# Second channel matmul of batch 1 in seven products of quarters, the u turns issued ahead of the last q turns, and a shifted PSUM bank count

## The chip, the cores and the metric

The kernel runs on one core of a Trainium2 chip. The metric is the device time of one execution in microseconds (us), as the median over several executions. The core's engines are called by the profile's names: PE (TensorE, matmuls) and PEld (its weight loads), DVE (VectorE), ACT (ScalarE), POOL (GpSimd) and SP (SyncE, which here only issues DMAs).

## What is computed

Eight batches, eight heads, 576 tokens, head size 64. A linear attention with cosine weights makes x; an MLP mixer with a token part and a channel part follows.

```python
q_p, k_p = phi(q), phi(k)             # relu(x) * cos_w and relu(x) * sin_w, side by side: 128 features
kv  = einsum('bhsf,bhsd->bhfd', k_p, v)
z   = sum(k_p, axis=2)
num = einsum('bhsf,bhfd->bhsd', q_p, kv)
den = einsum('bhsf,bhf->bhs', q_p, z)[..., None] + 1e-06
x   = (num / den).transpose(0, 2, 1, 3).reshape(8, 576, 512)
h   = maximum(x.transpose(0, 2, 1) @ w_tok1, 0) @ w_tok2      # 576 -> 256 -> 576
u   = x + h.transpose(0, 2, 1)
out = u + maximum(u @ w_ch1, 0) @ w_ch2                       # 512 -> 1536 -> 512
```

Inputs and output are float32; the matmuls take bfloat16 and add up in float32.

## The kernel before

**Groups and stages.** The 576 tokens of a batch are four blocks of 128 and a tail of 64. The MLP of a batch works on the four blocks (512 tokens); the eight tails of 64 make a ninth group (g = 8). A head part of the program does batch 0 and most of the work ahead of batch 1. Then comes the loop `for g in range(1, B + 1)` (L977), one **stage** for each group. In stage g, PE runs the channel MLP of group g. In between, the attention of batch b = g + 1 is finished, its token MLP is done, and the features of batch f = g + 2 are prepared.

**Steps.** The order of all instructions is written out by hand. `plan_of(g)` (L920) gives a list of steps, and `put(s, fn, ...)` hangs work on step s. Each step first issues a piece of the MLP on PE and then what hangs on it, in the order of the `put` calls. Steps 0 to 11 are the first channel matmul: one of twelve tiles of h1T (128 rows of the hidden layer by 512 tokens) with four matmuls of 512 columns (`mlp1`, L316), which `mlp1_out` (L328 on ACT, L330 on DVE) takes through relu into `h1T`. Every engine works through its own instructions in the order of the program; DMAs that SP issues wait in SP's order too.

**Second channel matmul, two forms.** In stage 1 (and for batch 0) it is plain: `mlp2` (L334) does, for each of four token blocks, twelve matmuls of 512 columns, in three steps of four, and `mlp2_out` (L339, DVE) adds u. From stage 2 on it has a form with seven products of quarters (Strassen's scheme in Winograd's form): the two dimensions h1T x w_ch2 are halved, `t_sum` makes T1 to T4 from the four quarters B11, B12, B21, B22 of w_ch2 once, `s_sums` makes S1 to S4 from the quarters of h1T in each stage (four DVE instructions for each range of chunks c, L358 to L361), and `mlp2_unit` (L378) does 14 units of six matmuls of 256 columns, two for each product. `mlp2_sums` adds the products up: a copy on ACT (L399), six additions on DVE (L401 to L430) and six additions of u on POOL (L396, in three pairs).

**Where S and T lie.** They use buffers of raw inputs that are free by then: S1 to S3 in `raw["k"][1]`, T3 and T4 in `raw["q"][1]`, S4 in `raw["v"][1]`. Batches 1 and 3 are the only ones loaded into the buffers [1]; all others go to [0].

**PSUM.** `psM` has four banks, handed out in turn by `nextM()` (count `cnt["M"]`), for MLP tiles and products; `psA` has two double banks for everything else.

**The turns.** Features of q (`qfeat`, L137 on ACT, L139 on DVE) are turned into `qpT` by a transposing DMA on SP (`qturn_dma`, L161), one for each of five token blocks j. u is cast to bfloat16 on ACT (`u_cast`, L264) and turned into `uT` by two such DMAs (`uturn_dma`, L269). All of `uT` of a batch must be there before the first MLP tile of its stage. For batch 1, ahead of the loop, u is turned on PE instead, into two psM banks, and copied out by DVE (`uturn_out`, L283, shown as L155). `tail_turn` (L304) turns the tails of u.

**Other work in the plan.** `f1k` makes one half of the K features of a block (which 0 with cos, 1 with sin) on a given engine; `vcast` casts v on POOL (L155); `kv_step` (L182) does kv for a block, `num_step` num (L201, L205) and x (L218 to L222), `b1_step` and `u_step` the token MLP (L232 to L259). `q_load`, `k_load`, `v_load` issue the loads of a later batch on SP (L131). `flush` issues the stores of results on POOL.

Of the kernel before, what the change touches and what calls it, by code (L numbers as in the profile page):

```python
# [18 lines left out]
def kernel(  # L19
# [77 lines left out]
    def views(t, m):  # L97
        b, n = t.rearrange("p h n d -> p (h n d)").bitcast(BF16), NQ * DQ
        return [b[:, i * n:(i + 1) * n].rearrange("p (c d) -> p c d", c=NQ) for i in range(m)]

    T1, T2 = [sb(f"w_ch2_t{i}", [P, NQ, DQ], BF16) for i in (1, 2)]
    T3, T4 = views(raw["q"][1], 2)
    S1, S2, S3 = views(raw["k"][1], 3)
    S4, = views(raw["v"][1], 1)
# [248 lines left out]
    def s_sums(c0, c1):  # L353
        V = nc.vector
        s1, s2, s3, s4 = [x[:, c0:c1, :] for x in (S1, S2, S3, S4)]
# [4 lines left out]
        V.tensor_sub(s3, a11, a21)  # L360
        V.tensor_sub(s4, a12, s2)  # L361
# [3 lines left out]
    def mlp2_unit(g, i):  # L365

        pr, tt = divmod(i, 2)
        a, w, bank = ((h1T[:, 0:NQ, 0:2 * P], B11, "A"), (S2, T2, "X"), (S3, T3, "F"), (S1, T1, "E"),
# [487 lines left out]
    uturn_out(1, 1, uturn_mm(1, nextM()), V)  # L856
    p(2, 3)
# [12 lines left out]
    order_of = lambda g: range(NCH) if g == 1 else (0, 6, 1, 7, 2, 8, 3, 9, 4, 5, 10, 11)  # L870
# [49 lines left out]
    def plan_of(g):  # L920
        b, f = g + 1, g + 2
        NS = 24 if g == 1 else 26
        plan = [[] for _ in range(NS)]

# [3 lines left out]
        if g == 1:  # L928
            put(5, tail_step, 1)
            put(19, tail_turn, 1)  # L930
            for j in range(NJ):
                put(j // 2 + 1, f1k, b, j, 0, V)
                put((j + 1) // 2 + 2, kv_step, b, j)
                put(5 + j, num_step, b, j)
            put(3, u_out, 1, 1)
            for n in range(2):
                put(10 + n, b1_step, b, n)
                put(13 + n, u_step, b, n)
                put(13 + n, uturn_step, b, n)
            for j in range(NJ):  # L940
                put(8 + j, f1k, f, j, 1, A)
                put(10 + j, f1k, f, j, 0, V)
                put(8 + j, vcast, f, j, G)
                put(18 + j, kv_step, f, j)
            for j, at in enumerate((12, 15, 16, 17, 18)):
                put(at, q_step, f, j)
            for i in range(4):
                put(19 + i, t_sum, i)
            put(8, v_load, 4)
            put(20, q_load, 4)  # L950
            put(22, k_load, 4)
            return plan
# [8 lines left out]
        for at, cs in ((7, (0, 2)), (9, (2, 4)), (11, (4, 5))):  # L961
            put(at, s_sums, *cs)
        if f < B:
            for j in range(NJ):
                put((7, 8, 10, 12, 13)[j], qfeat, f, j, V, A)
                put((7, 8, 10, 12, 13)[j], qturn_dma, f, j)
# [10 lines left out]
    for g in range(1, B + 1):  # L977
        mps = {}
        plan = plan_of(g)
        order = order_of(g)  # L980
        for s in range(len(plan)):
            if s < NCH:
                ps = mlp1(g, order[s])
            elif g == 1:
                t, part = divmod(s - NCH, 3)
                if part == 0:
                    mps[t] = nextM()
                mlp2(g, t, part, mps[t])
            else:
                mlp2_unit(g, s - NCH)  # L990
                mlp2_sums(g, s - NCH)
# [42 lines left out]
```

## Time and profile before

| what | value |
|---|---|
| median of 4 runs | 266.46 us (265.88, 266.26, 266.66, 267.33) |
| the profiled execution | 265.88 us, span from first to last instruction 264.1 us |
| granted PE clock | 1.00 throughout |
| stage 1, tiles of the first matmul | starts 57.81, ends 73.66 |
| stage 1, second matmul | 73.66 to 86.96 |
| first MLP tile of stages 4, 5, 6 | 140.17, 168.21, 195.86 |
| PE's last group of matmuls starts | 259.96 |

How to read the profile: times in a timeline are us from the start of the span; a line there gives start, duration, engine, source line, operation, written and read tiles, and how many instructions are merged in it. In brackets stands how long the engine had been idle before it, and what ended the wait. The wait table gives for engine and tile the releaser, the idle time in total, how many times, and the longest. "SPq" is SP's queue of DMA issues; there the duration is that of issuing. A line number can be that of a helper: every cast or copy on POOL or DVE has L155, every feature L137 or L139.

Busy time in a few stretches (us; of the stretch's length):

| stretch | PE | weight loads | DVE | ACT | POOL |
|---|---|---|---|---|---|
| 57.80 to 73.66 (stage 1, first half) | 15.79 of 15.86 | 7.98 | 12.25 | 9.02 | 4.25 |
| 73.66 to 86.96 (stage 1, second half) | 13.19 of 13.30 | 6.70 | 11.26 | 8.15 | 1.78 |
| 100.90 to 114.10 (stage 2, second half) | 13.20 of 13.20 | 10.44 | 11.61 | 9.10 | 5.08 |
| 140.00 to 168.00 (stage 4) | 26.89 of 28.00 | 17.03 | 23.42 | 18.10 | 11.90 |
| 168.00 to 196.00 (stage 5) | 26.48 of 28.00 | 17.19 | 21.45 | 16.75 | 10.24 |

### The profile page before, as it was taken

How to read it: one execution, taken by the hardware profiler on the slowest of the kernel's cores; microseconds unless marked ns; L12 is line 12 of the kernel's file. 1: busy time of each engine (PE TensorE's matmuls, PEld its weight loads, DVE VectorE, ACT ScalarE, POOL GpSimd, SP SyncE). 2: the span in 40 equal slices, each digit the busy share in tenths (PEclk: the TensorE clock that was granted, in tenths of full speed). 3: DMA queues.
4: the chain of work that ended last, by engine and by line, in shares of the span. 5: the costliest groups of instructions: out<-in, count | busy, mean ns of one | idle time of the engine just before them, and what ended most of it. 6: DMA issues, size and time to landing. Idle time of an engine off the chain costs nothing. (4 is left out here: it accounts for less than half of the span.)

```text
span 264.1 us, 5726 instructions
## 1 busy us (share of the span) xinstructions
PE 252.3 (96%) x2122; PEld 153.3 (58%) x2138; DVE 191.8 (73%) x447; ACT 148.4 (56%) x246; POOL 99.0 (37%) x172
## 2 busy tenths in 40 slices
PE   7799999989999999999999999899989999999994
PEld 2565456445445546864695468555855476486483
DVE  5883886696869689859985999398937783463563
ACT  4763685875666549646864687357825442612610
POOL 4196657070312510540545073604290135036032
PEclk9999999999999999999999999999999999999999
DMA  6999999999968999799968995899961035103004
GB/s 202 368 376 392 387 390 379 288 198 359 362 175 198 213 305 185 152 255 316 274 126 243 378 232 82 214 367 255 142 194 71 0 76 130 56 0 122 39 0 161
DMA packets 79948, 57.20 MB, mean 217 GB/s; under 512 B 48176, under 2 KB 74928, under 8 KB 79920
## 3 DMA queue, kind: packets, MB, share of 16 engines
q1 hardware_dynamic: 76128, 47.26, 67.3%
q0 software_dynamic: 2560, 8.39, 8.0%
q10 hardware_dynamic: 1232, 1.18, 1.4%
q8 instruction: 17, 0.28, 0.4%
q14 instruction: 11, 0.09, 0.1%
HBM read 35.85 MB, written 9.44 MB: 171 GB/s over the span
## 5 line engine op out<-in xcount | busy, mean ns | idle before, releaser
L316 PE MATMUL psM<-uT,w_ch 128*128 128x512 bf16 x368 | 88.2, 379 | 3.3 <-DMA uT<-u_bf 2.3
L328 ACT ACTIVATE h1T<-psM 128x512 bf16<-128x512 f32 x93 | 55.4, 597 | 45.5 <-PE psM L316 43.6
L316 PEld LDWEIGHTS <-w_ch 128*128 128x128 bf16 x416 | 37.5, 97 | 43.7 <-issue 5.0
L396 POOL TENSOR_TENSOR res<-res,u_sb 128x256 f32<-128x256 f32 x36 | 26.7, 772 | 52.5 <-DVE res L401 46.5
L155 POOL CAST vb<-v_raw 128x512 bf16<-128x512 f32 (+1 forms) x43 | 25.4, 633 | 52.8 <-DMA v_raw<-in_v_dram 52.5
L137 ACT ACTIVATE kp<-k_raw,sin_t 128x512 bf16<-128x512 f32 (+1 forms) x45 | 28.1, 666 | 1.3 <-DMA k_raw<-in_k_dram 1.3
L137 ACT ACTIVATE qp<-q_raw,sin_t 128x512 bf16<-128x512 f32 (+1 forms) x40 | 26.3, 681 | 2.8 <-DMA q_raw<-in_q_dram 2.8
L378 PEld LDWEIGHTS <-k_raw 128*128 128x128 bf16 x252 | 24.4, 98 | 5.1 <-issue 1.2
L378 PEld LDWEIGHTS <-h1T 128*128 128x128 bf16 x252 | 23.9, 98 | 5.3
L334 PE MATMUL psM<-w_ch,h1T 128*128 128x512 bf16 x90 | 22.7, 379 | 0.2
L139 DVE TENSOR_SCALAR kp<-k_raw,cos_t 128x512 bf16<-128x512 f32 (+1 forms) x45 | 21.0, 494 | 1.8 <-DMA k_raw<-in_k_dram 1.8
L378 PE MATMUL psM<-w_ch,h1T 128*128 128x256 bf16 x168 | 22.1, 273 | 0.0
L259 DVE TENSOR_TENSOR u_sb<-psA,x_sb 128x1024 f32<-128x1024 f32 x16 | 19.4, 1215 | 2.1 <-PE psA L254 1.9
L378 PE MATMUL psM<-w_ch_t,k_raw 128*128 128x256 bf16 x162 | 20.5, 273 | 0.0
L222 DVE TENSOR_TENSOR x_sb<-psA,rden 128x512 bf16<-128x512 f32 x28 | 19.4, 691 | 1.0
L358 DVE TENSOR_TENSOR k_raw<-h1T 128x512 bf16<-128x512 bf16 (+1 forms) x28 | 10.3, 370 | 11.8 <-ACT h1T L328 11.1
L139 DVE TENSOR_SCALAR qp<-q_raw,cos_t 128x512 bf16<-128x512 f32 (+1 forms) x40 | 17.3, 464 | 1.4 <-DMA q_raw<-in_q_dram 1.4
L218 DVE TENSOR_SCALAR rden<-psA 128x8 f32<-128x8 f32 x35 | 5.7, 163 | 16.2 <-PE psA L201 15.0
L254 PE MATMUL psA<-B,w_tok 128*128 128x512 bf16 x63 | 16.4, 379 | 0.1
L444 POOL DMA_DIRECT2D out_dram<-res x16 | 8.9, 558 | 19.5 <-DVE res L339 14.2
L201 PEld LDWEIGHTS <-qpT 128*128 128x128 bf16 x256 | 11.8, 98 | 7.6 <-issue 1.2
L232 PE MATMUL psA<-x_sb,w_tok 128*128 128x512 bf16 x50 | 14.1, 379 | 0.6 <-DVE x_sb L222 0.3
(139 smaller groups left out, 372.3 us busy)
## 6 DMA issues: line engine op xcount, KB each, us to landing
out_dram<-res POOLq DMA_DIRECT2D x32, 256.0 KB, 4.4
k_raw<-in_k_dram SPq DMA_DIRECT2D x7, 640.0 KB, 9.4
v_raw<-in_v_dram SPq DMA_DIRECT2D x7, 640.0 KB, 10.8
q_raw<-in_q_dram SPq DMA_DIRECT2D x7, 640.0 KB, 6.9
k_raw<-in_k_dram SPq DMA_DIRECT2D x7, 512.0 KB, 7.8
v_raw<-in_v_dram SPq DMA_DIRECT2D x7, 512.0 KB, 10.4
q_raw<-in_q_dram SPq DMA_DIRECT2D x7, 512.0 KB, 4.6
u_sb<-in_moe_w_ch_dram SPq DMA_DIRECT2D x2, 1024.0 KB, 10.2
```

The costliest lines, as they stand in the source:

```text
L137: eng.activation(out_ap, in_ap, AF.Relu, bias=0.0, scale=s)
L139: eng.tensor_scalar(out_ap, in_ap, scalar1=s, scalar2=0.0, op0=ALU.mult, op1=ALU.max)
L155: eng.tensor_copy(out_ap, in_ap)
L222: nc.vector.tensor_mul(dst.rearrange("p (g h d) -> p g h d", g=2, h=HH), n[:, :, :, 0:D], rb)
L232: nc.tensor.matmul(ps[mi], w1[:, j, mi * P:(mi + 1) * P], x_sb[:, j, :], start=(mi == 0 and j == 0), stop=(mi == 1 and j == T - 1), skip_g ...
L254: nc.tensor.matmul(ps[:, half, :], w2[:, ki, 2 * c + half, :], B1[b % 2][:, ki, :], start=(ki == 0), stop=(ki == NT - 1))
L259: nc.vector.tensor_add(u_sb[b % 2][:, 2 * c:2 * c + 2, :], ps, x_sb[:, 2 * c:2 * c + 2, :])
L316: nc.tensor.matmul(ps.rearrange("p (t k) -> p t k", k=P), wc1[:, ki, mi * P:(mi + 1) * P], src[:, :, ki, :], start=(ki == 0), stop=(ki == ...
L328: eng.activation(h1T[:, mi, :], ps, AF.Relu)
L334: nc.tensor.matmul(ps, h1T[:, ki, t * P:(t + 1) * P], wc2[:, ki, :], start=(ki == 0), stop=(ki == NCH - 1))
L378: nc.tensor.matmul(m[tt][:, tt, :], a[:, c, tt * P:(tt + 1) * P], w[:, c, :], start=(pr < 4 and c == 0 and (tt == 0 or own)), stop=(c == N ...
L396: G.tensor_add(c[:, t, :], s[:, t, :], u[:, t, :])
```

## The change

1. Stage 1 takes the form of seven products too: its plan grows from 24 to 26 steps, its first matmul follows the order of the other stages (0, 6, 1, 7, ...), the plain form of `mlp2` remains for batch 0 alone.
2. For that, T1 to T4 are made within stage 1 (steps 3, 4, 12 and 17, where they were at 19 to 22), T3 = B22 - B12 is written over B12, and S and T get other places: `rows_of(t, i)` takes a quarter-run of 256 elements out of each of six rows of a raw buffer and leaves the fifth block of a row alone. In stage 1, S1 and S2 lie in `raw["k"][0]` and S3 in `raw["q"][0]`; later in the buffers [1]. S4 and T4 lie in `raw["v"][1]` always.
3. Around it, the plan of stage 1 changes: `vcast` of batch 3 at step 5; K features with sin at 9 to 11; the turns of u at 15 and 16 (13 and 14 before); Q features and turns of batch 3 at 12, 13, 20, 21, 22 (12, 15 to 18 before), K features with cos at 15, 15, 19, 20, 21, both for blocks 0 and 1 on ACT instead of DVE; `kv_step` of batch 3 at 20, 21, 22, 24, 25; `q_load(4)` at 22 (20 before).
4. In stages 2 to 5, the DMAs that turn q blocks 3 and 4 go from steps 12 and 13 to step 17, behind the two turns of u at steps 15 and 16; their features stay where they were.
5. `cnt["M"] += 2` after the two turns of u for batch 1: every later tile takes the psM bank two further on.

```diff
-    def views(t, m):
-        b, n = t.rearrange("p h n d -> p (h n d)").bitcast(BF16), NQ * DQ
-        return [b[:, i * n:(i + 1) * n].rearrange("p (c d) -> p c d", c=NQ) for i in range(m)]
+
+    def rows_of(t, i):
+        b = t.rearrange("p h n d -> p h (n d)").bitcast(BF16)
+        return b[:, 0:NQ, i * DQ:(i + 1) * DQ]
 
     T1, T2 = [sb(f"w_ch2_t{i}", [P, NQ, DQ], BF16) for i in (1, 2)]
-    T3, T4 = views(raw["q"][1], 2)
-    S1, S2, S3 = views(raw["k"][1], 3)
-    S4, = views(raw["v"][1], 1)
+    T3 = B12
+    S4, T4 = [rows_of(raw["v"][1], i) for i in range(2)]
+    S_of = [[rows_of(raw["k"][i], 0), rows_of(raw["k"][i], 1), rows_of(raw["q"][i], 0), S4] for i in range(2)]
...
     uturn_out(1, 0, uturn_mm(0, nextM()), V)
     uturn_out(1, 1, uturn_mm(1, nextM()), V)
+    cnt["M"] += 2
     p(2, 3)
...
             put(3, u_out, 1, 1)
+            for i, at in enumerate((3, 4, 12, 17)):
+                put(at, t_sum, (0, 1, 3, 2)[i])
+            for j in range(NJ):
+                put((9, 10, 10, 11, 11)[j], f1k, f, j, 1, A)
             for n in range(2):
                 put(10 + n, b1_step, b, n)
                 put(13 + n, u_step, b, n)
-                put(13 + n, uturn_step, b, n)
+                put(15 + n, uturn_step, b, n)
+            put(10, s_sums, g, 0, 3)
+            put(11, s_sums, g, 3, 5)
             for j in range(NJ):
-                put(8 + j, f1k, f, j, 1, A)
-                put(10 + j, f1k, f, j, 0, V)
-                put(8 + j, vcast, f, j, G)
-                put(18 + j, kv_step, f, j)
-            for j, at in enumerate((12, 15, 16, 17, 18)):
-                put(at, q_step, f, j)
-            for i in range(4):
-                put(19 + i, t_sum, i)
+                put((12, 13, 20, 21, 22)[j], qfeat, f, j, (A, A, V, V, V)[j], A)
+                put((12, 13, 20, 21, 22)[j], qturn_dma, f, j)
+                put((15, 15, 19, 20, 21)[j], f1k, f, j, 0, (A, A, V, V, V)[j])
+                put(5, vcast, f, j, G)
+                put((20, 21, 22, 24, 25)[j], kv_step, f, j)
             put(8, v_load, 4)
-            put(20, q_load, 4)
+            put(22, q_load, 4)
             put(22, k_load, 4)
...
                 put((7, 8, 10, 12, 13)[j], qfeat, f, j, V, A)
-                put((7, 8, 10, 12, 13)[j], qturn_dma, f, j)
+                put((7, 8, 10, 17, 17)[j], qturn_dma, f, j)
...
             if s < NCH:
-                mlp1_out(order[s], ps, V if s in ((11,) if g == 1 else (10,)) else A)
-                if g > 1 and s == NCH - 1:
-                    s_sums(NQ - 1, NQ)
-            elif g == 1 and part == 2:
-                mlp2_out(g, t, mps[t], False)
+                mlp1_out(order[s], ps, V if s == 10 else A)
+                if s == NCH - 1:
+                    s_sums(g, NQ - 1, NQ)
```

More of the change, by code (lines that the diff above doesn't have):

```diff
@@ L351, in t_sum, with s_sums @@
             V.tensor_sub(T3, B22, B12)
-    def s_sums(c0, c1):
+    def s_sums(g, c0, c1):
         V = nc.vector
-        s1, s2, s3, s4 = [x[:, c0:c1, :] for x in (S1, S2, S3, S4)]
+        s1, s2, s3, s4 = [x[:, c0:c1, :] for x in S_of[min(g, 2) - 1]]
         a11, a21 = h1T[:, c0:c1, 0:2 * P], h1T[:, c0:c1, 2 * P:4 * P]
@@ L367, in mlp2_unit @@
         pr, tt = divmod(i, 2)
+        S1, S2, S3, S4 = S_of[min(g, 2) - 1]
         a, w, bank = ((h1T[:, 0:NQ, 0:2 * P], B11, "A"), (S2, T2, "X"), (S3, T3, "F"), (S1, T1, "E"),
@@ L866 @@
         load(3, src_of[n], n, (SY, SY))
-    order_of = lambda g: range(NCH) if g == 1 else (0, 6, 1, 7, 2, 8, 3, 9, 4, 5, 10, 11)
+    order = (0, 6, 1, 7, 2, 8, 3, 9, 4, 5, 10, 11)
     def kv_step(b, j):
@@ L921, in plan_of @@
         b, f = g + 1, g + 2
-        NS = 24 if g == 1 else 26
-        plan = [[] for _ in range(NS)]
+        plan = [[] for _ in range(26)]
         def put(s, fn, *args):
@@ L961, in plan_of @@
         for at, cs in ((7, (0, 2)), (9, (2, 4)), (11, (4, 5))):
-            put(at, s_sums, *cs)
+            put(at, s_sums, g, *cs)
         if f < B:
@@ L977 @@
     for g in range(1, B + 1):
-        mps = {}
         plan = plan_of(g)
-        order = order_of(g)
         for s in range(len(plan)):
@@ L983 @@
                 ps = mlp1(g, order[s])
[L984 to L988, printed above, removed]
             else:
```

## The prediction

> **What bounds the kernel now.** I read the busy shares first, then the waits of PE, then PE's timeline where it idles, and last the queues that set those idle moments.
>
> ```profile
> PE 252.3 (96%) x2122; PEld 153.3 (58%) x2138; DVE 191.8 (73%) x447; ACT 148.4 (56%) x246; POOL 99.0 (37%) x172
> PE psM L316 <- DMA uT<-u_bf: 2.3, 2, 1.3
> PE psM L316 <- DVE res L339: 0.7, 1, 0.7
> PE psM L316 <- DVE res L420: 0.2, 1, 0.2
> ```
>
> PE is busy 96% of the span, and from stage 1 on its only waits are these three, 3.2 us together (columns: sum, times, longest). So the time falls by what PE no longer has to issue and by these waits, and by little else. Where they lie:
>
> ```profile
> 57.81 2.75 PE L316 MATMUL psM<-uT,w_ch 128*128 128x512 bf16 x12 [0.73 <-DVE res L339]
> 140.17 2.75 PE L316 MATMUL psM<-uT,w_ch 128*128 128x512 bf16 x12 [0.21 <-DVE res L420]
> 168.21 2.75 PE L316 MATMUL psM<-uT,w_ch 128*128 128x512 bf16 x12 [1.09 <-DMA uT<-u_bf]
> 195.86 2.75 PE L316 MATMUL psM<-uT,w_ch 128*128 128x512 bf16 x12 [1.26 <-DMA uT<-u_bf]
> ```
>
> All stand at the head of a stage (1, 4, 5, 6), before its first MLP tile. The whole second half of stage 1 (73.66 to 86.96) runs without a wait.
>
> **The products (a gain of 1.19).** Stage 1 drops 48 matmuls of 512 columns and gets 14 units of six matmuls of 256, 84 in all. The chain of waits has both counts as uninterrupted runs:
>
> ```profile
> 231.91 9.17 PE psM L378 x84
> 241.08 10.36 PE psM L316 x48
> ```
>
> 10.36 - 9.17 = 1.19 us less on PE (216 against 109 ns each). The 36 further weight loads lie under matmuls: in the second half of stage 2, made of these units, PE's loads are busy 10.44 of 13.20 us, and PE is busy throughout.
>
> The Trainium skill has a rule against this edit: "TensorE: Matmul & The Clock Gate", section Back-to-back issue gap, says that in a stream of load and matmul a 512-column matmul costs about 131 ns and a 128-column one about 81, so halving the columns saves much less than half. By it (an estimate, 98 ns for 256 columns) the edit would be 84 x 98 - 48 x 131 = 1.9 us dearer. The trace's 216 and 109 ns contradict the rule, and I go by the trace.
>
> **The other bank (0.60).** Before stage 1, PE's last matmul of batch 0 ends at 57.08. The two copies of the turned u (DVE, 55.84 for 1.32) end at 57.16. Then comes L339, whose first addition frees the bank of tile 0, and PE starts at 57.81.
>
> ```profile
> 55.84 1.32 DVE L155 COPY uT<-psM 128x1024 bf16<-128x1024 bf16 x2
> 57.08 1.28 DVE L339 TENSOR_TENSOR res<-psM,u_sb 128x512 f32<-128x512 f32 x2
> ```
>
> With the count moved by two, tiles 0 and 1 take the banks of the turned u, free at 56.5 and 57.16. The start becomes 57.16 + 0.05 = 57.21, a gain of 0.60. The banks behind L339 now hold tiles 2 and 3, wanted at 58.9 and 59.8; L339 is done at 58.36. Late next is the K feature of batch 2 (DVE, 59.41 to 59.88), which PE wants at 59.81: 0.1 lost.
>
> **Turns of u before the last q turns (2.35).** Stage 5:
>
> ```profile
> 186.93 1.03 ACT L264 CAST u_bf<-u_sb 128x1024 bf16<-128x1024 f32 x1
> 188.49 1.03 ACT L264 CAST u_bf<-u_sb 128x1024 bf16<-128x1024 f32 x1
> 187.27 1.23 SPq L161 DMA_TRANSPOSE qpT<-qp  x1
> 189.19 1.23 SPq L161 DMA_TRANSPOSE qpT<-qp  x1
> 190.52 2.23 SPq L269 DMA_TRANSPOSE uT<-u_bf  x1
> 192.87 1.24 SPq L269 DMA_TRANSPOSE uT<-u_bf  x1
> ```
>
> The casts end at 187.96 and 189.52, but SP issues in order, and q turn 4 waited for its DVE feature until 189.19. The second u turn is issued at 192.87 and lands at 195.73 (2.86 later). Put first, it issues at 189.55 and lands at 192.4; PE is ready at 194.60. The wait of 1.26 goes, with 2.2 to spare. Likewise stage 4: casts end at 159.9 and 161.9, landing 164.7 against PE at 167.12; 1.09 goes. Stage 2 had no such wait. The 0.21 ahead of stage 4 is between nothing (bank) and 0.21 (that u turn, issued 137.27, lands near 140.1); I take nothing. What is late next is L416, which frees the bank of the next first tile: 193.41 + 0.61 = 194.02, in time by 0.6.
>
> The q turns themselves now go out at about 190.9 and 192.2 and land 3.0 to 6.5 later (the view of the q turns' line gives 4.2 as median), 198.7 at worst; PE wants turn 3 at 200.7 and turn 4 at 201.8. The q and v loads behind them in SP's queue leave at the same time as before, since the same four turns stand ahead. POOL's queue is untouched there. K loads, though, follow SP while the stages shrink, so they come up to 1.1 closer to their features; ACT is then late by at most that, within the 2.2 spare of the u turn.
>
> **Stage 1 rearranged (a loss of 0.7).** DVE gets 12 sums of quarters, six additions of 0.6 in place of four, and gives back four features to ACT. Its list from the end of the last x (70.32, which is 70.92 less 0.6): sums of chunks 0 to 2 1.96 (from 1.48 for a set of four at 512 columns and 1.0 at 256, in stage 2), MLP tile 0.61, sums 1.48 and 1.0, T3 and T4 0.95 each, two u 1.14 each, six additions 3.66, six features 2.4: 15.3, so to 85.6, where PE ends at 85.2. No slack is left, and POOL's casts of v sit on the first sums:
>
> ```profile
> 70.48 3.26 POOL L155 CAST vb<-v_raw 128x512 bf16<-128x512 f32 x5 [10.75 <-DMA v_raw<-in_v_dram]
> 155.16 0.69 DVE L360 TENSOR_TENSOR k_raw<-h1T 128x256 bf16<-128x256 bf16 x1
> 184.71 0.28 DVE L360 TENSOR_TENSOR k_raw<-h1T 128x256 bf16<-128x256 bf16 x1
> ```
>
> The same sum takes 0.28 alone and 0.69 under casts (152.29 to 155.7), 0.3 to 0.4 more. Four sums of stage 1 run under them: +1.4. Then S2 is whole at 76.35; PE reaches its last part in the second product at 75.8: 0.55 of wait. DVE stays late; the features for the K products of batch 3 come at 83.1, 83.9 and 85.3 against 83.0, 84.5 and 85.4: another 0.1 to 0.2. Bounds: nothing (sums at their own price) to 1.6 (every bf16 operation doubled). I take 0.7, the middle, since the row of 0.69 is the nearest.
>
> The Trainium skill, "SBUF — State Buffer", section SBUF: two separate sides, says that an operation with two SBUF inputs and a GpSimd operation lock each other out of a shared port for a whole instruction. By that four sums could each wait a full cast of 0.6, +2.4, an estimate 1.0 above mine. The row's 0.3 to 0.4 decides.
>
> S4 overwrites batch 3's v, so its first part waits for the casts of heads' blocks 0 and 1 (71.8), just when DVE reaches it at 71.8; behind it on DVE wait MLP tile 10 and all later sums. If it waits for all five casts (73.74), that is the same lateness, already under the casts, not a second one. The new views of S step by 640 elements from one chunk to the next with runs of 256; the sums' sources in h1T are read in the same way already, so I price them at the rows' own 0.28 and 0.41. Casts issued at step 5 cost nothing: POOL is idle, held by the v load until 70.48. T1 and T2 go into DVE's idle 2.33 ahead of 65.02 (0.95 and 1.52: 0.1 over, before a tail addition with slack). ACT gets four features (2.5) and one copy (0.5) where it is busy 8.15 of 13.30. Its second u cast comes at 82.0, the turn lands at 84.9, PE wants it at 85.7. The u turns now pass q turns 2 to 4 on SP, and SP then sends tail turn, q turns 2 to 4 and at about 88 the q load (91.36 before), so the 2.84 that ACT waited for q in stage 2 shrinks; off PE's path.
>
> **Sum.** 1.19 + 0.60 + 2.35 - 0.1 - 0.7 = 3.3. The profiled execution took 265.88 (span 264.1 and 1.8 around it): 262.6. The median of the runs shown, 266.46, is 0.6 above it: 263.1. I put 263.0.
>
> **Rivals.** About 0.5%, 1.33 us, is what a measurement tells from no change; the line is at 265.1.
> (a) DVE becomes the bound of stage 1: all sums and T's doubled, 1.6 at the sums, then a late u turn and K features, 1 more: loss 2.6 for 0.7, time 264.9 at worst, 264.4 typical. For: a list as long as the stage. Against: half of it reads PSUM or meets no cast. 0.15.
> (b) The u turns were hidden anyway: their place is taken by the K load or by L416 and L420, and 2.35 is not gained: 265.4, no change. For: DMA is 88 to 98% busy in stages 4 and 5. Against: 2.2 spare. 0.11.
> (c) Slower: q turns 3 and 4 come too late. Place: the fourth and fifth numerators of stages 3 to 6. The tail turn of u, behind loads, took 11.7 to land; a q turn as slow would land at 203.9, 2.1 late, four times 8.4: 271.4. It costs from a landing of 9.6 on and makes the kernel slower (over 267.8) from 10.8. Against: the loads stand behind the turns, and 6.5 is the longest of 30. 0.06.
> (d) The stage 1 edit does not shorten PE (units stall on S and T as much as they save): 264.2. 0.06.
>
> My forecast: 0.62, own range 262.0 to 264.0. Range: down to 261.5 (no loss in stage 1, 0.21 and a low run), up to 265.3 for (a), (d) and most of (b). Faster 0.82, same 0.11, slower 0.07.
>
> **What would show it.** PE's L378 count up by 84 and L334 down by 48; stage 1's second half near 12.9; no wait on uT at stages 5 and 6, none on L339 at stage 1. Wrong if PE waits on DVE sums in stage 1 for over 1.6, on uT at stage 2, or on q turns at the numerators.

## The result and the profile after

The changed kernel takes 267.29 us (median of 43 runs) against 266.37 for the kernel before (64 runs): a ratio of 1.0029, 95% interval 1.0018 to 1.0041. The forecast was 263.0, with 265.3 as the end of its range. A few executions fall into a slower state; they are left out of the ratios, but not of the medians. The profiled execution has a span of 265.4 (before 264.1). First the page's busy shares, then the waits of PE (sum, times, longest):

```profile
PE 251.9 (95%) x2160; PEld 156.1 (59%) x2174; DVE 197.8 (75%) x457; ACT 151.6 (57%) x251; POOL 104.0 (39%) x178
```

```profile
PE psA L183 <- DVE kp L140: 1.2, 3, 0.7
PE psM L380 <- ACT h1T L329: 0.8, 2, 0.6
PE psM L380 <- DVE k_raw L360: 0.8, 1, 0.8
...
PE psM L380 <- DVE v_raw L350: 0.2, 1, 0.2
```

The waits that the change went for are gone: none on uT, none on L339 or L420. In their place stand four kinds that the kernel before did not have: on features of K (line 140), on a sum S (360), on T4 (350), and on MLP tiles from ACT (329). The line numbers are those of the changed kernel, one or two above those of before.

Stages, from the start of PE's first MLP tile in the timeline to the next one's:

| stage | 1 | 2 | 3 | 4 | 5 | 6 | rest |
|---|---|---|---|---|---|---|---|
| starts, before | 57.81 | 86.96 | 113.71 | 140.17 | 168.21 | 195.86 | 221.39 |
| starts, after | 57.79 | 89.20 | 117.42 | 143.51 | 170.47 | 196.63 | 222.16 |
| length, before | 29.15 | 26.75 | 26.46 | 28.04 | 27.65 | 25.53 | 42.7 |
| length, after | 31.41 | 28.22 | 26.09 | 26.96 | 26.16 | 25.53 | 43.2 |

Stages 3 to 5 give 2.94, but not all of it is the u turns' (run 2 below). Stage 1 loses 2.26 and stage 2 loses 1.47. Stage 1 starts no earlier, although its wait for L339 (0.73) is gone: in this execution PE's first transposes, in code that is the same, start 0.57 later (8.24 against 7.67). Counted from them, stage 1 starts 0.59 earlier (after 49.55 in place of 50.14), as the prediction's 0.60 for the bank has it. The first transposes start between 7.67 and 8.90 in the profiles shown here, so lengths of stages are compared below, and times by their medians.

The timeline of the changed kernel where stages 1 and 2 lose it (start, duration, engine; in brackets the idle time before it and what ended it):

```profile
70.56 3.82 POOL L156 CAST vb<-v_raw 128x512 bf16<-128x512 f32 x5 [10.25 <-DMA v_raw<-in_v_dram]
71.22 0.92 DVE L359 TENSOR_TENSOR k_raw<-h1T 128x768 bf16<-128x768 bf16 x1
72.17 0.85 DVE L360 TENSOR_TENSOR k_raw<-k_raw,h1T 128x768 bf16<-128x768 bf16 x1
...
77.81 0.28 PE L380 MATMUL psM<-w_ch_t,k_raw 128*128 128x256 bf16 x1 [0.81 <-DVE k_raw L360]
...
81.97 5.24 POOL L398 TENSOR_TENSOR res<-res,u_sb 128x256 f32<-128x256 f32 x6 [7.60 <-DVE res L403]
...
84.73 1.04 DVE L140 TENSOR_SCALAR kp<-k_raw,cos_t 128x512 bf16<-128x512 f32 x1
85.82 0.42 PE L183 MATMUL psA<-vb,kp 128*128 128x65 bf16 x8 [0.75 <-DVE kp L140]
86.55 0.94 DVE L140 TENSOR_SCALAR kp<-k_raw,cos_t 128x512 bf16<-128x512 f32 x1
88.02 0.47 DVE L140 TENSOR_SCALAR qp<-q_raw,cos_t 128x512 bf16<-128x512 f32 x1
88.94 0.42 PE L183 MATMUL psA<-vb,kp 128*128 128x65 bf16 x8 [0.32 <-DVE kp L140]
...
91.90 2.60 SPq L132 DMA_DIRECT2D q_raw<-in_q_dram  x2
101.36 0.72 ACT L138 ACTIVATE qp<-q_raw,sin_t 128x512 bf16<-128x512 f32 x1 [4.29 <-DMA q_raw<-in_q_dram]
104.20 0.71 PE L380 MATMUL psM<-w_ch,h1T 128*128 128x256 bf16 x5 [0.56 <-ACT h1T L329]
```

Three things are to be seen. DVE's first sums run under POOL's five casts, and PE then stands 0.81 for the last part of S2. DVE's features take 1.04 and 0.94 while POOL adds (81.97 to 87.21) and 0.47 once POOL is done (88.02); PE waits for them. And ACT waits 4.29 for batch 4's q (2.84 before); the MLP tiles queue behind the q feature on ACT, so PE waits for a tile at 104.20.

Without stalls the second half of stage 1 would be 13.30 - 1.19 = 12.11; it is 15.24 (73.96 to 89.20). Of the 3.13 between, 1.14 are lost up to the third product (79.45; run 3 needs 4.35 to that point, which after 73.96 would give 78.31), and 1.99 after it.

### The profile page after: what moved, and what is told of

Same layout as the page of the kernel before. It is cut to its first block, busy times and chain, and to the rows that moved or that the text cites. A ratio compares the mean times of both kernels' runs of the same rounds, so it can differ in the third digit from the quotient of the medians.

```text
span 265.4 us, 5823 instructions
## 1 busy us (share of the span) xinstructions
PE 251.9 (95%) x2160; PEld 156.1 (59%) x2174; DVE 197.8 (75%) x457; ACT 151.6 (57%) x251; POOL 104.0 (39%) x178
## 4 chain that ended last, share of the span: by engine, by line
PE 59%; ACT 0%; DVE 0%; issue 0%
PE psM L380 24%; PE psM L317 24%; PE psA L255 3%; PE psA L233 3%; PE psA L183 2%; PE psA L202 1%; PE psA L296 1%; PE psA L206 1%; PE psA L380 0%; PE psA L237 0%; ACT h1T L329 0%; DVE res L429 0%; PE psA L238 0%
## 5 line engine op out<-in xcount | busy, mean ns | idle before, releaser
L398 POOL TENSOR_TENSOR res<-res,u_sb 128x256 f32<-128x256 f32 x42 | 31.8, 789 | 61.2 <-DVE res L403 55.3
L380 PEld LDWEIGHTS <-h1T 128*128 128x128 bf16 x288 | 27.3, 98 | 7.4 <-issue 1.2
L380 PE MATMUL psM<-w_ch,h1T 128*128 128x256 bf16 x192 | 25.4, 273 | 0.8 <-ACT h1T L329 0.8
L380 PE MATMUL psM<-w_ch_t,k_raw 128*128 128x256 bf16 x186 | 23.9, 273 | 0.8 <-DVE k_raw L360 0.8
L380 PEld LDWEIGHTS <-k_raw 128*128 128x128 bf16 x192 | 18.4, 98 | 6.2 <-DVE k_raw L360 1.4
L359 DVE TENSOR_TENSOR k_raw<-h1T 128x512 bf16<-128x512 bf16 (+2 forms) x31 | 11.9, 384 | 11.9 <-ACT h1T L329 11.1
L193 ACT CAST kv_sb<-psA 128x520 bf16<-128x520 f32 x7 | 4.2, 604 | 18.4 <-PE psA L183 18.4
L183 PE MATMUL psA<-vb,kp 128*128 128x65 bf16 x280 | 13.3, 193 | 1.2 <-DVE kp L140 1.2
```

Source lines behind the costliest of these rows:

```text
L183: nc.tensor.matmul(ps[:, h // HH, (h % HH) * E1:(h % HH + 1) * E1], kp[j][:, h, :, :].rearrange("p a d -> p (a d)"), vb[j][:, h, 0:E1], st ...
L380: nc.tensor.matmul(m[tt][:, tt, :], a[:, c, tt * P:(tt + 1) * P], w[:, c, :], start=(pr < 4 and c == 0 and (tt == 0 or own)), stop=(c == N ...
L398: G.tensor_add(c[:, t, :], s[:, t, :], u[:, t, :])
```

## The experiments

All ratios are to the kernel before, with 95% intervals; the kernel before was timed beside each group. They are grouped by what they ask; the numbers in brackets give the order in which they ran, by which the expectations name them.

### The parts alone

**Turns and bank without the products** (1). The kernel before with two edits:

```diff
+    cnt["M"] += 2
...
-                put((7, 8, 10, 12, 13)[j], qturn_dma, f, j)
+                put((7, 8, 10, 17, 17)[j], qturn_dma, f, j)
```

> The kernel before with two parts of the change alone: the q turns 3 and 4 of stages 2 to 5 behind the u turns, and the shifted bank count. Theory (these two parts keep their gain, and what the change loses it loses in stages 1 and 2): no wait on uT at stages 4 to 6, none on L339 at stage 1, stages 3 to 5 shorter by 2.8 us together and stage 1 starting 0.6 earlier; about 263.1 us against 266.4 of the kernel before, ratio 0.988. Rival (the waits come back elsewhere once stage 1 ends earlier, because loads and SP's order pace the stages): 265 to 266 us.

Measured 265.51, ratio 0.9950 (0.9931 to 0.9969): the rival's number, and 1.3 of the 2.95 that these two steps were worth in the prediction. No wait on uT or L339 is left, but PE waits elsewhere. The timeline of this kernel in stage 5:

```profile
182.42 3.07 POOL L155 CAST vb<-v_raw 128x512 bf16<-128x512 f32 x5 [11.46 <-DMA v_raw<-in_v_dram]
183.10 0.69 DVE L360 TENSOR_TENSOR k_raw<-h1T 128x256 bf16<-128x256 bf16 x1
...
191.20 0.67 DVE L405 TENSOR_TENSOR res<-psM,res 128x512 f32<-128x512 f32 x1
191.93 0.81 PE L378 MATMUL psM<-q_raw,h1T 128*128 128x256 bf16 x6 [0.88 <-DVE res L405]
```

The casts of v start 14.4 after the stage (182.42 against 168.0; before 12.8) and meet five sums of 256 columns, which take 0.58 to 0.73 in place of 0.28. DVE's list ends late, and the addition L405 takes the place of the u wait: 0.88 here, 0.22 in stage 4. (That these sums are what makes L405 late is read from the timeline; no run tests it by itself.) Stages 3 to 5 are 80.52 together, 1.63 less than before. Stage 2 is 27.50, 0.75 longer than before.

**The bank alone** (10). The kernel before with

```diff
+    cnt["M"] += 2
```

> Kernel before with the other bank alone. Prediction's step: stage 1 starts 0.60 earlier and everything follows, 265.8 (ratio 0.9977). Rival: the 0.60 is given back, because stage 2 is paced by the load of batch 4's q, whose place does not move with PE, and the waits for uT at the heads of stages 5 and 6 stay as they are: 266.3, ratio 0.999 to 1.001. The rest of the 1.33 that both edits gave together belongs then to the u turns.

Measured 266.86, ratio 1.0000 (0.9972 to 1.0028). The rival holds: the bank is worth nothing by itself. Its profile has no wait on L339, and stage 1 starts 49.55 after the first transposes, 0.59 earlier than before, but stage 1 is 29.47 (0.32 more) and stage 2 is 28.02 (1.27 more), with ACT waiting 4.15 for q. The load of q also lands later here, counted from the first transposes: after 90.99 in place of 89.94. Why it does so no run shows.

**The products alone** (2). The changed kernel with both edits undone:

```diff
-    cnt["M"] += 2
...
-                put((7, 8, 10, 17, 17)[j], qturn_dma, f, j)
+                put((7, 8, 10, 12, 13)[j], qturn_dma, f, j)
```

> The changed kernel without those two parts: the seven products of batch 1 and the new plan of stage 1 alone. Theory: stage 1's second half near 15.2 us (13.3 before), stage 2 near 28.2 (26.75 before), so 3.4 us above the kernel before: about 269.8 us, ratio 1.013. Rival (the products gain their 1.2 us and the loss in the changed kernel comes from the parts acting together): at or under 266.4 us.

Measured 268.57, ratio 1.0065 (1.0040 to 1.0091), between the theory and the rival. Stages 1 and 2 are 31.83 and 27.94, about as long as the theory has them. But stages 3 to 5 are 80.31 together without any u turn moved, 1.84 less than before: PE comes to them 4.2 later, the wait on uT ahead of stage 5 is gone, and this is left of the 1.26 ahead of stage 6:

```profile
198.18 2.75 PE L317 MATMUL psM<-uT,w_ch 128*128 128x512 bf16 x12 [0.44 <-DMA uT<-u_bf]
```

So the product edit loses some 1.7, and the turns and the bank give about 1.0 with it (1.0065 to 1.0029) and 1.3 without. Of the 2.94 that stages 3 to 5 give in the changed kernel, these two edits have 1.10.

### What makes DVE late in stage 1

**POOL's casts left out** (3). The changed kernel without the casts of batch 3's v in stage 1 (vb of that batch is not written).

```diff
-                put(5, vcast, f, j, G)
```

> The changed kernel with the five POOL casts of batch 3's v in stage 1 left out (batch 3 then uses an older v). Theory (DVE is late in stage 1 because the first sums share time with POOL's casts and the fourth waits for them): the four sums of 768 columns take about 0.55 us each, 2.0 together from first start to the tile after them where it was 3.7, the wait of 1.15 us in the second product goes, and stage 1's second half falls from 15.2 to about 14 us. Rival (DVE has simply too much work there, whatever POOL does): the second half stays over 14.9 us.

Measured 265.26, ratio 0.9928 (0.9896 to 0.9960). Its timeline:

```profile
71.04 0.55 DVE L359 TENSOR_TENSOR k_raw<-h1T 128x768 bf16<-128x768 bf16 x1
71.62 0.56 DVE L360 TENSOR_TENSOR k_raw<-k_raw,h1T 128x768 bf16<-128x768 bf16 x1
72.10 0.55 DVE L361 TENSOR_TENSOR q_raw<-h1T 128x768 bf16<-128x768 bf16 x1
72.57 0.55 DVE L362 TENSOR_TENSOR v_raw<-h1T,k_raw 128x768 bf16<-128x768 bf16 x1
```

Four sums in 2.1 in place of 3.75 (71.22 to 74.97, of which 0.51 is the fourth's wait for a cast, since S4 lies over v). Stage 1 falls from 31.41 to 29.06, and its second half is 12.90 (13.30 before): the 12.9 that the prediction named. The features under POOL's additions still take 1.04, 0.95 and 0.94 here, but PE loses only 0.74 ahead of the kv steps (by the starts of its matmuls), since DVE comes to them 2.4 earlier in the stage.

**POOL's additions left out** (4). The changed kernel without the six additions of u in stage 1 (that part of the result is not added).

```diff
         def add_u(c, s, u):
+            if g == 1:
+                return
```

> The changed kernel with the six POOL additions of u in stage 1 left out (three quarters of batch 1's output lack their terms). Theory (POOL's additions slow the K and Q features on DVE from 0.47 to 0.95 us and T4 from 0.95 to 1.25): the features between 84 and 88 us take 0.47 each, PE's waits for the K features (0.75 and 0.32) go, and stage 1's second half falls from 15.2 to about 14.1 us. Rival (the features are slow for another reason, such as ACT's features of the same blocks or DMA): they stay near 0.95 us and the second half over 14.9.

Measured 266.82, ratio 1.0005 (0.9977 to 1.0032). The features:

```profile
84.55 0.48 DVE L140 TENSOR_SCALAR kp<-k_raw,cos_t 128x512 bf16<-128x512 f32 x1
84.94 0.48 DVE L140 TENSOR_SCALAR qp<-q_raw,cos_t 128x512 bf16<-128x512 f32 x1
```

0.48 each in place of 1.04 and 0.95, and stage 1 is 29.70. But stage 2 grows to 29.25, so most of the gain is given back there. Both POOL causes are shown, and a third one behind them. The two don't add: runs 3 and 4 take 2.35 and 1.71 off stage 1, together more than the 3.13 that were lost.

**K's features to ACT, ahead of its other work** (7). The changed kernel with

```diff
-                put((15, 15, 19, 20, 21)[j], f1k, f, j, 0, (A, A, V, V, V)[j])
+                put((15, 15, 14, 14, 14)[j], f1k, f, j, 0, A)
```

> The changed kernel with the last three K features with cos of batch 3 on ACT at step 14 of stage 1, where ACT idles 2.0 us, instead of DVE at steps 19 to 21. Theory (these features wait in DVE's late list and share time with POOL's additions): PE's waits for the K features (0.75 and 0.32) go, stage 1's second half falls from 15.2 to about 14.0 us and the q features on DVE come 2.4 us earlier, so that the q load is issued earlier too and stage 2 shrinks by up to 1; about 265.5 us. Rival (ACT becomes late instead: the u cast behind these features delays the turn of u): a wait on uT at the head of stage 2 and no gain.

Measured 267.12, ratio 1.0026 (0.9995 to 1.0056): the rival holds, there is no gain. Stage 1 falls to 30.08, but the second u cast stands behind three features on ACT (PE waits 0.42 for uT), and a q turn issued at 89.08 lands 7.5 later (1.84 of wait): stage 2 is 28.74.

**S2 and S4 out of the casts' way** (12). The changed kernel; the casts were given a later step too:

```diff
-    S_of = [[rows_of(raw["k"][i], 0), rows_of(raw["k"][i], 1), rows_of(raw["q"][i], 0), S4] for i in range(2)]
+    S_of = [[rows_of(raw["k"][0], 0), rows_of(raw["q"][0], 1), rows_of(raw["q"][0], 0), rows_of(raw["k"][0], 1)],
+            [rows_of(raw["k"][1], 0), rows_of(raw["k"][1], 1), rows_of(raw["q"][1], 0), S4]]
...
-            for i, at in enumerate((3, 4, 12, 17)):
+            for i, at in enumerate((3, 4, 12, 18)):
...
-                put(5, vcast, f, j, G)
+                put(13, vcast, f, j, G)
...
-            put(22, k_load, 4)
+            put(25, k_load, 4)
```

> Changed kernel, with POOL's five casts of batch 3's v at step 13 in place of 5, stage 1's S2 and S4 in batch 4's q and k buffers in place of batch 2's k and batch 3's v (so that no sum waits for a cast), T4 at step 18, and the k load of batch 4 at step 25. Theory: the lateness of DVE in stage 1 starts with the first sums under the casts; they take 0.55 each as with the casts left out (stage 1 29.06 there), the 0.51 wait is gone, and stage 1 is 29.5 to 30.3 in place of 31.41; the k load leaves the q load alone, some 0.5 in stage 2: 265.2 to 266.2. Rival: the casts are only moved onto other work (T3, the u additions, POOL's six additions behind them), so the lateness comes back before the K features: stage 1 at 31 and 267.3.

Measured 266.10, ratio 0.9964 (0.9943 to 0.9984). In its timeline the casts did not move:

```profile
71.86 4.14 POOL L157 CAST vb<-v_raw 128x512 bf16<-128x512 f32 x5 [10.49 <-DMA v_raw<-in_v_dram]
```

A later step holds nothing back on an engine that has nothing ahead of it: POOL still starts as the v load lands. The k load goes out right behind the q load, as it did. So this run shows the buffers and T4's place alone: the time is the theory's, but not by the theory's cause. The 0.51 wait is gone, T4 takes 0.95 in place of 1.25 (at 83.15), and stage 1 is 30.24, 1.17 less.

### What sets stage 2

**The load of q earlier** (5). The changed kernel with

```diff
-            put(22, q_load, 4)
+            put(18, q_load, 4)
```

> The changed kernel with the q load of batch 4 at step 18 of stage 1 instead of 22, ahead of the tail turn and of q turns 2 to 4 in SP's queue. Theory (stage 2 is long because this load lands late: ACT waits 4.3 us for it, and the MLP tiles queued behind on ACT come late for the first product): the load is issued near 85 instead of 91.9 us, ACT's wait for it goes, PE's three waits of 0.8 us at the first product of stage 2 go, and stage 2 falls from 28.2 to about 26.8 us; the time from 267.3 to about 266. Rival (the q turns, now behind the load, land late and PE waits at the numerators of stage 2 instead): stage 2 stays over 27.9 us, with waits on the q turns.

Measured 269.92, ratio 1.0149 (1.0101 to 1.0198). The rival holds. (The runs spread from 268.2 to 272.1 and the profiled one is the fastest: its stages 1 and 2 are only 0.7 longer than the changed kernel's, so the profile does not account for the whole loss.) ACT and DVE wait for q no more, but the q turns stand behind the load on SP, and the timeline has a new wait:

```profile
97.49 0.42 PE L202 MATMUL psA<-kv_sb,qpT 128*128 128x65 bf16 x8 [1.98 <-DMA qpT<-qp]
```

**The same without the products** (6). The first kernel (turns and bank) with

```diff
-            put(20, q_load, 4)
+            put(12, q_load, 4)
```

> The kernel before with the u turns first and the shifted bank count, as in the earlier run, and the q load of batch 4 at step 12 of stage 1 instead of 20. Theory (there the gain of the bank, 0.6 us, was given back in stage 2, 27.5 us long instead of 26.75, because the q load of batch 4 lands no earlier than before): no wait for q on ACT or DVE in stage 2, stage 2 at 26.7 us or less, the whole about 0.8 us under the 265.5 of the run without the earlier load. Rival (stage 2 is long for its stage 1 lateness on DVE): stage 2 stays at 27.3 or more and the time at 265.5.

Measured 267.11, ratio 1.0024 (1.0000 to 1.0049). Stage 2 is 26.74 now, so the load had been what paced it. But the u turns (issued 79.07 and 80.55) land 6.7 and 8.3 later, 2.8 before, and stage 1 is 31.48: PE waits 1.84 for uT.

**All of it together** (8). The changed kernel with the features of run 7 and the buffers of run 12, T1 moved to the head, and

```diff
-            put(10, s_sums, g, 0, 3)
+            put(4, s_sums, g, 0, 2)
+            put(10, s_sums, g, 2, 3)
...
-            put(22, q_load, 4)
-            put(22, k_load, 4)
+            put(18, q_load, 4)
+            put(25, k_load, 4)
```

> The changed kernel with all of it: q load at step 18, K features with cos on ACT at step 14, T1 made ahead of stage 1, the sums of chunks 0 and 1 at step 4 before the v casts arrive, and S2 and S4 of stage 1 in other free buffers so that no sum waits for a v cast (the k load of batch 4 then goes to step 25). Theory (all losses of the change lie in DVE's list in stage 1 and the late q load): stage 1's second half about 12.5 us, stage 2 about 26.8, stages 3 to 5 as in the changed kernel: about 262.5 to 263.5 us. Rival (loads pace the later stages, so what stages 1 and 2 give is taken back by DVE's waits in stages 4 and 5, as in the run of the two small parts): 264.5 to 265.5 us.

Measured 273.83, ratio 1.0279 (1.0241 to 1.0317). DVE was mended: PE was ready for stage 2 at 86.07, 28.49 after stage 1's start (29.15 before), though uT kept it until 87.32. But a q turn landed 11.1 after its issue:

```profile
99.41 0.62 PE L203 MATMUL psA<-kv_sb,qpT 128*128 128x65 bf16 x8 [7.12 <-DMA qpT<-qp]
```

**The stores held back** (11). The changed kernel; stage 1's four stores go out at step 6 of stage 2.

```diff
-                stores.append(lambda: store(g, 3, res[1]))
+                (held if g == 1 else stores).append(lambda: store(g, 3, res[1]))
...
-            stores.append(lambda: store(g, 1, res[0]))
+            (held if g == 1 else stores).append(lambda: store(g, 1, res[0]))
...
-            flush()
+            if (g, s) == (2, 6):
+                stores.extend(held)
+            flush()
```

> Changed kernel, with the four stores of stage 1's results issued at step 6 of stage 2 in place of the end of stage 1. Theory: the load of batch 4's q competes with 1 MB of stores that leave together at 90.4 to 92.6; without them it lands about 2 earlier (99.3 in place of 101.4), ACT waits some 2 in place of 4.29, and stage 2 is about 27.0 in place of 28.22: 266.1, ratio to before 0.999. Rival: the load is late because of its own issue and of the k load that follows it, not of the stores: landing 101, stage 2 28.2, 267.3, ratio 1.003.

Measured 267.66, ratio 1.0023 (0.9991 to 1.0055): by the time the rival's number, by the trace the theory's mechanism. The load lands 6.3 after its issue (92.12 to 98.46) in place of 9.5, and stage 2 is 26.74. But stage 1 is 32.69:

```profile
87.50 3.62 POOL L156 CAST vb<-v_raw 128x512 bf16<-128x512 f32 x5
...
89.07 0.83 DVE L140 TENSOR_SCALAR kp<-k_raw,cos_t 128x512 bf16<-128x512 f32 x1
89.95 0.42 PE L183 MATMUL psA<-vb,kp 128*128 128x65 bf16 x8 [0.98 <-DVE kp L140]
```

The stores, which wait on POOL for DVE's last additions, had kept the next batch's casts (92.61 in the changed kernel) away from stage 1's features. Without them the casts run at 87.50, under these. That is 0.66 of the 1.28 that stage 1 grows (0.98 in place of 0.32). Another 0.59 is a wait on a sum that comes ahead of the stores: the casts of batch 3's v start 0.6 later in the stage here (13.36 after its start, 12.77 in the changed kernel), and S4 waits 1.07 for them in place of 0.51.

**The tail's turn behind the loads** (15). The ninth kernel (next part) with

```diff
-            put(19, tail_turn, 1)
+            put(23, tail_turn, 1)
```

> The ninth kernel (before with the u turns ahead, the other bank, and K's cosine rows 2 and 3 on ACT from stage 2 on; 264.78), with the tail's turn of stage 1 at step 23 in place of 19, behind the loads of batch 4's q and k on SP. Theory: stage 2 is paced by the q load, whose issue stood behind the tail's turn (issued 90.97, 2.12 to the load's issue at 93.14); the load goes out and lands 2 earlier, stage 2 falls from 27.50 to 26.75, 264.1, ratio 0.990. Rival: the load then runs with the last two q turns and makes these late, as when it was moved to steps 12 and 18 (PE waits on qpT at a numerator), 265 or above.

Measured 263.53, ratio 0.9879 (0.9841 to 0.9917), the lowest median of all, though its interval overlaps those of runs 13 and 14. The load is issued 2.3 after the stage's start in place of 5.0, and stage 2 is 26.78:

```profile
88.96 2.02 SPq L131 DMA_DIRECT2D q_raw<-in_q_dram  x2
...
97.37 0.72 ACT L137 ACTIVATE qp<-q_raw,sin_t 128x512 bf16<-128x512 f32 x1 [2.91 <-DMA q_raw<-in_q_dram]
```

Stage 2 is what the theory has. Stage 5 is shorter too, 26.83 for 27.71 in run 9, which the theory doesn't explain.

The kernel before has these two rows:

```profile
91.36 1.32 SPq L131 DMA_DIRECT2D q_raw<-in_q_dram  x2
97.61 0.72 ACT L137 ACTIVATE qp<-q_raw,sin_t 128x512 bf16<-128x512 f32 x1 [2.84 <-DMA q_raw<-in_q_dram]
```

The runs together give the law of stage 2. "Landed" is the start of ACT's first feature of this q, "late" its distance from the start of stage 2. All runs in which ACT waits for this load are in it:

| kernel | q load issued | landed | stage 2 starts | late | stage 2 |
|---|---|---|---|---|---|
| stores held | 92.12 | 98.46 | 90.21 | 8.25 | 26.74 |
| held pair (13) | 90.36 | 98.20 | 87.82 | 10.38 | 26.74 |
| before | 91.36 | 97.61 | 86.96 | 10.65 | 26.75 |
| tail's turn late | 88.96 | 97.37 | 86.65 | 10.72 | 26.78 |
| features behind (14) | 91.42 | 99.50 | 88.56 | 10.94 | 27.00 |
| turns and bank | 92.16 | 98.68 | 87.25 | 11.43 | 27.50 |
| features late (9) | 93.14 | 99.62 | 88.18 | 11.44 | 27.50 |
| casts later | 91.51 | 100.62 | 89.09 | 11.53 | 27.59 |
| products alone | 92.45 | 101.81 | 89.93 | 11.88 | 27.94 |
| casts out | 89.24 | 98.61 | 86.68 | 11.93 | 28.00 |
| bank alone | 92.20 | 99.09 | 87.12 | 11.97 | 28.02 |
| after | 91.90 | 101.36 | 89.20 | 12.16 | 28.22 |
| features ahead (7) | 90.43 | 100.32 | 87.64 | 12.68 | 28.74 |
| additions out | 92.19 | 100.98 | 87.79 | 13.19 | 29.25 |

Up to 10.7 the load costs nothing; from there on the stage is 26.75 plus the excess, within 0.04 (in runs 4 and 7 PE waits for a q turn in this stage as well). The kernel before stands just at the knee. Whatever brings PE to stage 2 sooner without the load is given back in full: that is where the gain of the kernel without additions went, and what stage 1 left of the bank's. Runs 6, 11 and 15 are the test: each brings the load sooner, and stage 2 is 26.74 to 26.78.

### Versions with the collisions taken apart

**K's features of rows 2 and 3 on ACT from stage 2 on** (9). The first kernel (turns and bank) with

```diff
-                put((12, 13, 14, 15, 17)[j], f1k, f, j, 0, V)
+                put((12, 13, 17, 17, 17)[j], f1k, f, j, 0, (V, V, A, A, V)[j])
```

> Kernel before with the u turns ahead and the other bank (as in the first experiment, 265.51, 1.33 under before), and from stage 2 on the cosine features of K, rows 2 and 3, given from DVE to ACT at step 17. Theory: in the first experiment DVE's list took the place of the u wait in stages 4 and 5; PE waited 0.22 + 0.88 there for the addition L405. With two features of about 0.95 less on DVE both waits go: 1.1 less, 264.4, and stages 4 and 5 together 53.4 in place of 54.43. Rival: ACT has no room; the features or MLP tiles behind them come late on ACT, PE waits for kp or h1T instead, 265.5 or above. Second rival: it is the instruction order on DVE, not its load, that is late, and 0.88 stays.

Measured 264.78, ratio 0.9929 (0.9904 to 0.9953). The expected 264.4 is inside, but so is the first kernel's ratio, and the profile doesn't carry the theory: stages 4 and 5 are 54.87 (expected 53.4), with 0.27 on L405 and 0.41 + 0.27 on h1T. With the tail's turn moved, the same order gives 53.79 and 0.38 on L405. How much these two features are worth stays open.

**The products with the collisions taken apart** (13). The kernel of run 12 with the edit of run 9 and, of the stores of run 11, the second pair alone held (the first pair keeps the casts back):

```diff
-            stores.append(lambda: store(g, 1, res[0]))
+            (held if g == 1 else stores).append(lambda: store(g, 1, res[0]))
```

> The same without the move of batch 3's features: twelfth kernel, second pair of stores held, K's cosine rows 2 and 3 on ACT from stage 2 on. Theory: stage 1 stays at 30.2 (the casts of batch 4's v keep their gate, the first pair of stores, and so do not run under stage 1's features as they did with all four stores held); the q load competes with half the stores and lands about 1 earlier, stage 2 27.0 in place of 27.59; 265.4, ratio 0.995. Rival: half the stores slow the load as much as all, or the casts move up all the same: 266.1, ratio 0.997.

Measured 263.89, ratio 0.9895 (0.9858 to 0.9933), faster than the theory's 265.4, though stage 1 is longer than it has it. Stage 1 is 30.59 (0.81 on a sum and 0.47 + 0.32 on features are left), stage 2 26.74, the load landing 10.38 after its start; stages 4 and 5 are 52.84 (53.57 in run 12).

**The same, with batch 3's last three features on ACT behind its other work** (14):

```diff
-                put((15, 15, 19, 20, 21)[j], f1k, f, j, 0, (A, A, V, V, V)[j])
+                put((15, 15, 16, 22, 22)[j], f1k, f, j, 0, A)
```

> The twelfth kernel (S2 and S4 of stage 1 moved, T4 at step 18, k load at 25) with three more edits: batch 3's three cosine features of K that DVE had go to ACT, row 2 at step 16 behind the second u cast, rows 3 and 4 at step 22 behind the sine features of q; of stage 1's stores the second pair is held to step 6 of stage 2; from stage 2 on K's cosine rows 2 and 3 are on ACT. Theory (what is left of stage 1's lateness are the DVE features doubled under POOL's additions, and the late q load follows from them, since its issue stands behind q turns that wait for those features): no PE wait on kp (0.47 and 0.32 go), q turns issued about a microsecond earlier, stage 1 29.3 to 29.8 in place of 30.24, stage 2 26.7 to 27.2 in place of 27.59: 263.3 to 264.5, ratio 0.988 to 0.992. Rival: ACT is the one that is late now, as when all three features stood ahead of the u casts (second u turn or a q turn late, PE waits on uT or qpT): 266 or above.

Measured 264.29, ratio 0.9887 (0.9847 to 0.9927). Stage 1 falls to 29.75 and stage 2 is 27.00 (the load 10.94 late), both as expected. By the time it is no different from the kernel without this move, so what this move saves in stage 1 can't be told in the time.

## Why the prediction was wrong

The number was 4.3 too low, and the sign was wrong. By its own steps, with profiled lengths:

- **The products, 1.19: right, but hidden.** With the casts out, the second half of stage 1 is 12.90. PE loses 0.74 of it ahead of three kv steps, which leaves 12.16, near the 12.11 of the forecast.
- **The other bank, 0.60: the step that failed in its direction.** The start was right (0.59 earlier), the gain is not there. Alone it measured 1.0000: 0.32 went in stage 1 (I had 0.1) and, by the law above, the rest in stage 2, where the load of q moreover landed later by itself.
- **"The 2.84 that ACT waited for q in stage 2 shrinks; off PE's path": the step that failed in kind.** It grew to 4.29 and was on PE's path from 10.7 on. The text had the load going out at about 88; it went at 91.90, and then took 9.5 beside four stores. Ahead of it on SP the second u turn went out at 83.44 (the text has its cast at 82.0), the first of the last three q turns waited for its DVE feature until 86.78, and these three took 5.02 to issue. Cost: 1.47. I had read the trace of before as if a wait of ACT with no wait of PE meant slack; it was at the knee.
- **"Stage 1 rearranged (a loss of 0.7)": mis-sized.** 3.13 in place of 0.7. The sums cost 1.14 (I had 0.55). Of the other 1.99, by the starts of its matmuls PE loses 1.56 ahead of three kv steps that want features (I had 0.1 to 0.2) and 0.38 ahead of the product that wants T4. I gave six features 2.4 at their own price and looked for POOL only at the sums, though the form of seven products brings six additions on POOL into this stage too. The 0.51 wait of S4 was named and taken as covered; it came on top.
- **Turns of u, 2.35: right in place, mis-sized.** The waits at stages 5 and 6 are gone. But stages 3 to 5 are only 1.63 shorter in run 1, where L405 took back 1.1 (rival (b) had other work take the place of the turns, but named L416, L420 and the K load). The 2.94 of the changed kernel is luck in part: by run 2, 1.84 of it come without the turns, as PE is late anyway.
- **The rivals.** (a), DVE as the bound of stage 1, is the one that came, at 0.15, but its price of 2.6 at worst was too small, and it missed stage 2. (d), that the units stall as much as they save, holds for the products by themselves, at a higher price than it named. (c) did not come in stages 3 to 6; turns that land late because of a load are real (7.12 of wait in one kernel), where a load is moved ahead of them.

Added up: start 0.02 gained (0.59 by the bank, 0.57 lost in the head), stage 1 2.26 lost, stage 2 1.47 lost, stages 3 to 5 2.94 gained, the rest 0.5 lost, is 1.3, the difference of the spans. The head's 0.57 and the 0.5 at the end are not the change's doing as far as the profiles show: the 0.5 lies behind DVE's last addition (which ends 3.0 before the end of the span before, 3.6 after), where only stores land. Without both the two profiles differ by 0.2 and the medians by 0.9; the rest stays open. With the collisions taken apart the forecast time is nearly met (263.89 with the products, 263.53 without; the kernel before took 266.95 beside them). So the products themselves don't decide: what they save on PE in stage 1 they cost in waits there, in every run that left no work out. Run 8 comes nearest, with PE ready after 28.49 and then kept by uT.

The Trainium skill, "SBUF — State Buffer", section SBUF: two separate sides, calls the port that DVE and GpSimd share an exclusive lock held for a whole instruction. I had set it aside for the 0.3 to 0.4 of one row. The runs fit it: under POOL's additions, one every 0.87 (5.24 / 6), features start 0.95 and 0.87 apart; under casts, one every 0.61 (3.07 / 5), sums of 256 columns start 0.66, 0.61 and 0.61 apart (run 1). In these rows one DVE operation passes for each POOL operation, though alone it takes 0.47 or 0.28. It doesn't hold for all: DVE's additions that read PSUM keep their pace (L413 starts at 84.13, the feature behind it at 84.73), and T4 (0.95 alone) takes 1.25 under the additions in the changed kernel, but 0.95 under them in runs 3 and 12.

## What to carry to other kernels

Price a short operation of DVE from SBUF to SBUF that runs under POOL's work at the period of POOL's operations, and look at every POOL operation of the stage, those that the change adds included. A wait of an engine off the path is slack only as far as a run has shown it: move the consumer earlier, and the load behind it becomes the bound. Before a transfer is moved, count what stands ahead of it and behind it in its queue; taking one transposing DMA out of the load's way was worth more here than any move of the load itself.

## What the runs showed of the hardware

- In stage 1 of the kernels before and after, with no load of q just ahead of them on SP, u turns landed 2.7 to 3.6 after their issue and q turns 3.1 to 6.1. Behind that load (1152 KB) u turns took 6.7 and 8.3 (run 6), and q turns 5.0 to 6.7 (run 5) and 11.1, 9.5 and 5.9 (run 8). A q turn that went out 1.35 ahead of the load took 7.5 (run 7).
- The load of q landed 6.3 after its issue without stores beside it (run 11), and 9.5 after it with four stores (256 KB each) leaving in the same 2 us (the changed kernel). With two stores it was 6.3 to 6.9 when the first went out 3 to 4 us ahead of the load (before, runs 1, 9 and 10) and 7.8 to 8.4 when it went out 1 to 2 us ahead (runs 13 to 15).
- In the stall of 7.12 (92.3 to 99.41 in run 8) the granted clock fell. The view of windows of that kernel (from and to, sum, then busy times of PE, PEld, DVE, ACT and POOL, the clock, DMA share, GB/s):

```profile
90.00:94.00 4.00, 2.28 (x25) 1.08 (x23) 2.12 (x6) 1.79 (x3) 3.10 (x6) 1.00 1.17 273
94.00:96.00 2.00, 0.00 (x0) 0.00 (x0) 0.00 (x0) 0.00 (x0) 0.00 (x0) 0.77 1.11 128
96.00:98.00 2.00, 0.00 (x0) 0.00 (x0) 0.00 (x0) 0.00 (x0) 0.00 (x0) 0.50 1.13 203
...
100.00:102.00 2.00, 2.00 (x14) 0.92 (x12) 1.06 (x3) 0.17 (x1) 0.00 (x0) 0.50 0.86 159
```

The clock was 1.00 before the stall and still 0.50 after PE had work again (until 105). So this wait cost more than its length: stage 2 took 36.77 in this run, which is 26.75, the wait of 7.12 and 2.9 more.
